# One load per group for plain v from batch 1 on, and a later place for the transposed remainders and the copies of even blocks' keys

## The chip, the cores and the metric

The kernel runs on one core of one Trainium2 chip. The core has five engines with a queue of instructions each, which they work off in order and independently of each other: TensorE (PE in the profile; its weight loads are PEld), VectorE (DVE), ScalarE (ACT), GpSimd (POOL) and SyncE (SP, which here only issues transfers). Semaphores order what one engine writes and another reads. The metric is the device time of one execution in microseconds (us), taken as the median over runs; lower is better.

## The reference

There are 8 batches, 8 heads, 576 positions and a head size of 64. Half of the heads attend to the last 32 positions ("plain"), the other half to every fourth of the last 128 ("dilated"):

```python
rel = pos[:, None] - pos[None, :]
mask_plain = (rel >= 0) & (rel < window)                              # window = 32, heads 0 to 3
mask_dil = (rel >= 0) & (rel < window * dilation) & (rel % dilation == 0)   # dilation = 4, heads 4 to 7
attn = softmax(where(mask, q @ k.T / sqrt(64), -1e9)) ; x = heads of attn @ v side by side (8, 576, 512)
gate = sigmoid(causal depthwise convolution of x, 5 taps, conv_w (5, 512))
out = (gate * (x @ w_val)) @ w_out                                    # w_val, w_out (512, 512)
```

Inputs and output are float32; the kernel works in bf16 on PE.

## The kernel before, in words

**Steps and groups.** The main loop has 32 steps `i`, four for each batch `b`. One step takes two heads of one batch; `c` (0 to 3) is the step in the batch. Steps with `c` 0 and 1 are plain, `c` 2 and 3 dilated (`dil`). Two steps of a kind form a group `g`, 16 in all; `a` is 0 in the first step of a group and 2 in the second. The lines below are those of the kernel before.

**What a step does.** The order of instructions is written out by hand in the loop (L805 to L879), and each engine keeps it; the first seven steps (`EARLY = 7`) have an order of their own in `early_rest` (L754). In a step: `scores(i, 0)` and `scores(i, 1)` (PE L494 for plain steps, L511 for dilated ones; then exp on ACT, L514); the convolution of an earlier step (PE L639, its gate on ACT L648); `apply_mask` for both halves (DVE L523), with `after_x(i-1)` between them, which transposes the normalised output of the step before (PE L593, L600, L606; DVE L608); the transposes of k or q of the next group (`trans_main`, PE L405 or L413; copied out by ACT L425 to L439); `attn_v` (PE L544 or L558); `normalize` (DVE L573, L574; L580, L581 in the first five steps); and, spread between these, value products (`run_val`: PE L664 or L659, DVE L670) and output tiles (`run_out`: PE L700, ACT L704, stores by SP L710).

**Memory for results of PE.** From step 5 on the second half of a step's scores and its attention output use the same tile `ps_sc`; there are two such tiles, so the second half of the next step's scores waits until `normalize` (L574) has read it. All else goes through four banks `ps_bank`, used in turn.

**Remainders.** A sequence has 576 = 512 + 64 positions. The main part is transposed by `trans_main`; the last 64 positions of q and k are loaded apart and transposed by `trans_rest` (two PE transposes L455; DVE copies L463 and L466 for plain groups, L473 and L475 for dilated ones). In the main loop that is done in the first step of a group, and in step 7, for the group after it, right behind `normalize`.

**Plain keys.** A plain step splits the 576 queries into six blocks of 96. A block needs its 96 keys and the 32 before them; PE takes them in two strided halves `j`. An odd block reads 128 consecutive columns of `kT`. An even block reads them likewise in batches below `FB`; from batch `FB` on it reads `kE`, in which the 96 keys of the block stand first and the 32 earlier ones behind (L490, L491). `even_keys` (L443) fills `kE` for three even blocks with two DVE copies: L447 (96 keys of each) and L448 (the 32 earlier ones of two of them; the first block has none). It depends on the main part of k alone: the columns that it reads end at 480.

**Plain v.** In batches below `FB` v is loaded by `load_v_half` (L152) in the layout of the blocks, with an overlap, 128 partitions wide: two transfers for each pair of heads. POOL then casts it to bf16 in one instruction (L219). From `FB` on v is loaded once, 96 partitions wide (L175), and POOL casts it in four pieces (L223 to L226) which move the partitions to where the blocks want them. `mask_f` and `mask_p` are the masks for the two layouts. `prep_v` does the casts; for the steps around the change POOL's order is: in step 3 `cast_val` and `prep_v(4)`, in step 4 `prep_v(5)`, `cast_out` and `prep_v(6)`, in step 5 `prep_v(7)`, in step 6 eight casts of `swap_out`.

**Loads.** SP issues all but the first few loads in program order, far ahead: in step 0 the first pair of group 2 (batch 1, plain), in step 1 its second pair, in steps 2 and 3 group 3 and group 4.

Of the kernel before, what the change touches and what calls it, by code (L numbers as in the profile page):

```python
# [15 lines left out]
def hi_bf16(ap: bass.AP) -> bass.AP:  # L16

    b = ap.bitcast(BF16)
    idx = tuple([slice(None)] * (len(b.shape) - 1) + [slice(1, None, 2)])
    return b[idx]  # L20
# [3 lines left out]
def kernel(  # L24
# [11 lines left out]
    nc = tc.nc  # L36

    B, H, S, D = q.shape
# [10 lines left out]
    NB = 6  # L49
    AVS = 72  # L50
    HB = 288
    KOFF = 32
# [33 lines left out]
    kTs = [consts.tile([128, 2, KOFF + S], BF16, name=f"kT{i}") for i in range(NKT)]  # L86

    kEs = [consts.tile([128, 2, NB // 2, 128], BF16, name=f"kE{i}") for i in range(NKT)]
    FB = 2
    NET = 2  # L90
    ets = [consts.tile([128, 2, 2 * HB + 96], BF16, name=f"et{i}") for i in range(NET)]
    NVP = 2
# [1 line left out]
    vPs = [consts.tile([128, 4, NB, 66], BF16, name=f"vP{i}") for i in range(NVP)]  # L94
# [21 lines left out]
    def bank_b():  # L116
        return bank().bitcast(BF16).rearrange("p (z n) -> p z n", z=2)
# [51 lines left out]
    def load_v(g, a=0, e=4, eng=nc.sync):  # L169
        b, dil = g // 2, g % 2  # L170
        t = grp_tiles.setdefault(g, {})
        if not dil and b >= FB:

# [36 lines left out]
    def prep_v(i):  # L210
# [3 lines left out]
        if not dil:  # L214
            w = vPst[b % NVP][:, a * NB // 2:e * NB // 2, :].rearrange(
                "p (h u) (j d) -> p h (u j) d", u=NB // 2, j=2)
            x = vPs[b % NVP][:, a:e, :, 0:D]
            if b < FB:
                nc.gpsimd.tensor_copy(x, w)  # L219
# [14 lines left out]
    def pair_info(i):  # L234
        b, c = i // NCH, i % NCH
        dil = int(c >= NCH // 2)
        return b, c, dil, 2 * b + dil, (c % 2) * 2
# [45 lines left out]
        nc.vector.memset(et[:, :, 2 * HB:], 1.0)  # L283
    for i in range(NVP):
        nc.vector.memset(vPs[i][:, :, :, D:D + 1], 1.0)
        if i == 0:
            nc.vector.memset(vPst[i][0:16, 0, :], 0.0)

# [76 lines left out]
    def make_conv_diag(c):  # L365
        nc.vector.tensor_tensor(
            out=conv_diag[:, c, :, :],
            in0=ident_h[:, None, :].to_broadcast([128, K, D]),
            in1=conv_w_sb[:, c, :, None].to_broadcast([128, K, D]),
            op=ALU.mult)  # L370
# [69 lines left out]
                    out=t["kB"][:, 2 * z0:2 * z1, 0:TM - TB, :],  # L440
                    in_=src.rearrange("p z (h w t) -> p (z h) t w", h=2, w=2)[:, :, TB:TM, :])

    def even_keys(g):  # L443
        t = grp_tiles[g]
        ke = t["kE"] = kEs[(g // 2) % NKT]
        kt = t["kT"][:, :, KOFF:KOFF + S].rearrange("p z (u s) -> p z u s", u=NB // 2)
        nc.vector.tensor_copy(ke[:, :, :, 0:96], kt[:, :, :, 0:96])  # L447
        nc.vector.tensor_copy(ke[:, :, 1:NB // 2, 96:128], kt[:, :, 0:NB // 2 - 1, 160:192])  # L448

    def trans_rest(g):  # L450
        dil = g % 2
        t = grp_tiles[g]
        ps = bank_b()
        for z in range(2):
            nc.tensor.transpose(  # L455
                out=ps[:, 0, TM * z:TM * z + TM],
                in_=hi_bf16(t["rest"][:, z, :]), identity=ident)
        pk, pq = ps[:, 0, 0:TM], ps[:, 0, TM:2 * TM]
        if not dil:
            if "qT" not in t:  # L460
                t["qT"] = qt_pool.tile([128, 2, DIL, T], BF16, name="qT")
            t["kT"] = kTs[(g // 2) % NKT]
            nc.vector.tensor_copy(  # L463
                t["kT"][:, :, KOFF + RM:KOFF + S], pk.rearrange("p (s z) -> p z s", z=2))
            for z in range(2):
                nc.vector.tensor_copy(  # L466
                    t["qT"][:, z, :, TM:T],
                    pq.rearrange("p (t r z) -> p z r t", r=DIL, z=2)[:, z])
        else:
            t["qB"] = qt_pool.tile([128, 4, 2, TR], BF16, name="qB")  # L470
            if "kB" not in t:
                t["kB"] = qt_pool.tile([128, 4, 64, 2], BF16, name="kB")
            nc.vector.tensor_copy(  # L473
                t["kB"][:, :, TM - TB:64, :], pk.rearrange("p (t w h) -> p h t w", h=4, w=2))
            nc.vector.tensor_copy(t["qB"], pq.rearrange("p (t w h) -> p h w t", h=4, w=2))  # L475
# [4 lines left out]
    def scores(i, hf):  # L480
# [3 lines left out]
        for n in range(3):  # L484
            if not dil:
                u, j = (3 * hf + n) // 2, (3 * hf + n) % 2
                for z in range(2):
                    m = 2 * u + z
                    kk = t["kT"][:, a // 2, 96 * m + j:96 * m + j + 127:2]
                    if z == 0 and b >= FB:  # L490
                        kk = t["kE"][:, a // 2, u, j:128:2]  # L491
# [25 lines left out]
    def apply_mask(i, hf):  # L517
        b, c, dil, g, a = pair_info(i)
        et = st[(i, "et")]
        e3 = et[:, hf, 0:2 * HB].rearrange("p (h n) -> p h n", h=2)  # L520
        m = mask_d if dil else (mask_f if b < FB else mask_p)[:, 3 * hf:3 * hf + 3, :].rearrange("p n q -> p (n q)")
        m = m[:, None, :].to_broadcast([128, 2, HB])
        nc.vector.tensor_tensor(out=e3, in0=e3, in1=m, op=ALU.mult)  # L523
# [195 lines left out]
    def run_conv(i):  # L719

        while convs and convs[0][0] < i:
            conv(*convs.pop(0)[1])

    def run_val():
        item = vals.pop(0)
        while item not in gates:
            conv(*convs.pop(0)[1])
        val(*item)
        G = item[2]
        done_val[G] += 1  # L730

        while HB * (done_val[G] // NCH) >= 128 * (done_out[G] + 1):
            outs.append((G, done_out[G]))
            done_out[G] += 1
# [8 lines left out]
    EARLY = 7  # L743

    def next_pair(i, names=("k", "q", "rest")):

        g, z = (i + 1) // 2, (i + 1) % 2
        for name in names:
            if name != "rest":
                trans_main(g, name, (z,))  # L750
            elif z == 0:
                trans_rest(g)

    def early_rest(i):  # L754

        if i == 0:
            setup_conv_w()
            make_conv_diag(0)
            warm(3)
        run_conv(i - 1)  # L760
        apply_mask(i, 0)
        if i == 0:
            make_conv_diag(1)
        if i > 0:
            after_x(i - 1)
        apply_mask(i, 1)
        if i == 0:
            make_conv_diag(2)
            next_pair(i, ("k",))
        elif i < NCH:  # L770
            next_pair(i)
        if i < NCH:
            warm(2)
        else:
            run_val()
        attn_v(i, 0)
        attn_v(i, 1)
        if i == 0:
            next_pair(i, ("q",))
        normalize(i)  # L780
        if i == 0:
            make_conv_diag(3)
        if i < NCH:
            warm(1)
        else:
            run_val()
            next_pair(i)
        if i == 5:
            run_val()
            run_val()  # L790
        elif i == 6:
            run_out()
            trans_main(4, "k")
            run_out()
# [10 lines left out]
    for i in range(NP):  # L805
        b, c, dil, g, a = pair_info(i)

        if i == 0:
            load_weight(0, moe_w_val)
            load_pair(2, 0)  # L810
        elif i == 1:
            load_pair(2, 2)
        elif i == 2:
            load_weight(1, moe_w_out)
            load_pair(3, 0)
        elif i == 3:
            load_pair(3, 2)
            load_group(4)
        if c % 2 == 0 and 5 <= g + 3 < 2 * B:
            load_group(g + 3)  # L820

        if i == 0:
            prep_v(0)
            make_mask_d()
            prep_v(1)
            make_perm()
        elif i < 3:
            prep_v(i + 1)
            if i == 2:
                make_mask_p()  # L830
        elif i == 3:
            cast_val()
            prep_v(4)
        elif i == 4:
            prep_v(5)
            cast_out()
            prep_v(6)
        elif i == 5:
            prep_v(7)
        elif i == 6:  # L840
            for m in range(NCH):
                for h in range(2):
                    swap_out(h, m)
        elif i > 6:
            if i < NP - 1:
                prep_v(i + 1)
            if g + 2 < 2 * B and g % 2 == 0:
                cast(g + 2, "k" if a == 0 else "q")
            if 9 <= i < 13:
                swap_val(i - 9)  # L850
        scores(i, 0)
        scores(i, 1)
        if i < EARLY:
            early_rest(i)
            continue
        run_conv(i - 1)
        apply_mask(i, 0)
        after_x(i - 1)
        if g + 1 < 2 * B:
            trans_main(g + 1, "k" if a == 0 else "q")  # L860
        apply_mask(i, 1)
        if c == 0 and outs:
            run_out()
        elif vals:
            run_val()
        attn_v(i, 0)
        attn_v(i, 1)
        normalize(i)
        if (a == 0 or i == EARLY) and g + 1 < 2 * B:
            trans_rest(g + 1)  # L870
            if dil:
                even_keys(g + 1)
        if c == 0 and vals:
            run_val()
        for _ in range((2 if len(outs) > 2 else 1) - (c == 0 and i > NCH)):
            if outs:
                run_out()
        if vals:
            run_val()  # L879
    run_conv(NP - 1)  # L880
    if outs:
        run_out()
# [36 lines left out]
```

## Time and profile before

| what | us |
|---|---|
| median of 13 runs (lowest, highest) | 180.41 (178.81, 182.33) |
| the profiled execution, whole time | 179.82 |
| its span in the profile | 177.9 |
| busy in it: PE, DVE, ACT, POOL | 162.2, 124.8, 114.0, 94.5 |
| L447, the 96 keys of each even block: least, median, most of 6 | 0.298, 0.427, 0.535 |
| L448, the 32 earlier keys of two blocks: least, median, most of 6 | 0.177, 0.184, 0.830 |
| four partial casts of v for one step, from 47.50 to 50.74 | 3.24 |
| the one cast of v for a step of batches 0 and 1 | 0.82 |

The span runs from the first to the last instruction that the profiler saw; the whole time has 1.9 us around it. The median of the runs stands 0.59 us above the profiled execution. A row of slices shows 40 equal parts of the span, 4.45 us each, in tenths. In the rows of the time line, the first number is the start within the span, the second the length of that group of instructions; "[0.36 <-ACT et L514]" says that the engine stood idle for 0.36 us before it, and what ended that. In the list of waits the numbers are the sum, how often, and the longest.

### The profile page before, as it was taken

How to read it: one execution, taken by the hardware profiler on the slowest of the kernel's cores; microseconds unless marked ns; L12 is line 12 of the kernel's file. 1: busy time of each engine (PE TensorE's matmuls, PEld its weight loads, DVE VectorE, ACT ScalarE, POOL GpSimd, SP SyncE). 2: the span in 40 equal slices, each digit the busy share in tenths (PEclk: the TensorE clock that was granted, in tenths of full speed). 3: DMA queues.
4: the chain of work that ended last, by engine and by line, in shares of the span. 5: the costliest groups of instructions: out<-in, count | busy, mean ns of one | idle time of the engine just before them, and what ended most of it. 6: DMA issues, size and time to landing. Idle time of an engine off the chain costs nothing.

```text
span 177.9 us, 7022 instructions
## 1 busy us (share of the span) xinstructions
PE 162.2 (91%) x2911; PEld 108.5 (61%) x2911; DVE 124.8 (70%) x314; ACT 114.0 (64%) x215; POOL 94.5 (53%) x164
## 2 busy tenths in 40 slices
PE   6879779789969899999999999999999999999991
PEld 2445547576546665667766676677677766665540
DVE  4397726776478798789878876887597959773330
ACT  3337724656867766777877778777967796564340
POOL 7373761559698994799069839923788100000000
PEclk9999966999999999999999999999999999999998
DMA  5999999999999999979999999999997222224355
GB/s 149 234 258 346 330 203 244 336 270 250 272 332 249 326 338 314 186 209 336 288 254 307 326 318 248 310 296 292 260 331 244 64 63 63 61 63 105 94 165 169
DMA packets 49274, 42.27 MB, mean 238 GB/s; under 512 B 6885, under 2 KB 43733, under 8 KB 49242
## 3 DMA queue, kind: packets, MB, share of 16 engines
q1 hardware_dynamic: 48544, 41.36, 86.3%
q8 instruction: 22, 0.36, 0.9%
q10 hardware_dynamic: 698, 0.47, 0.8%
q14 instruction: 10, 0.08, 0.2%
HBM read 32.38 MB, written 9.44 MB: 235 GB/s over the span
## 4 chain that ended last, share of the span: by engine, by line
PE 69%; DVE 11%; DMA 10%; ACT 4%; SPq 3%; issue 1%; ACTq 0%; DVEq 0%
PE ps_bank L700 16%; PE ps_bank L664 14%; PE ps_bank L639 11%; DMA q_nat<-in_q_dram 10%; PE ps_bank L413 5%; DVE et L523 4%; PE ps_sc L544 4%; PE ps_sc L494 3%; PE ps_sc L558 3%; PE ps_sc L511 2%; PE ps_bank L593 2%; DVE xn L574 2%; DVE xT L608 2%; PE ps_bank L606 2%; ACT et L514 1%; SPq L127 1%
## 5 line engine op out<-in xcount | busy, mean ns | idle before, releaser
L514 ACT ACTIVATE et<-ps_sc 128x576 bf16<-128x576 f32 x64 | 38.3, 648 | 16.6 <-PE ps_sc L494 11.7
L704 ACT ACTIVATE osb<-ps_bank 128x512 f32<-128x512 f32 x35 | 21.4, 611 | 25.0 <-PE ps_bank L700 18.6
L670 DVE SCALAR_TENSOR_TENSOR y<-gate,ps_bank 128x288 bf16<-128x288 bf16 x64 | 28.3, 449 | 10.2 <-PE ps_bank L664 7.6
L639 PE MATMUL ps_bank<-xT,conv_diag 64*64 64x288 bf16 (+1 forms) x768 | 27.7, 270 | 0.1
L574 DVE TENSOR_TENSOR xn<-ps_sc,rec 128x768 bf16<-128x768 f32 (+1 forms) x27 | 25.8, 955 | 0.9
L648 ACT ACTIVATE gate<-ps_bank 128x288 bf16<-128x288 f32 x64 | 23.1, 423 | 2.0 <-PE ps_bank L639 1.9
L523 DVE TENSOR_TENSOR et<-et,mask_d 128x576 bf16<-128x576 bf16 x32 | 16.6, 520 | 7.0 <-ACT et L514 7.0
L639 PEld LDWEIGHTS <-conv_diag 64*64 64x64 bf16 x768 | 19.1, 108 | 3.1 <-DVE qB L475 0.8
L664 PE MATMUL ps_bank<-xT,w_val_b 128*128 128x288 bf16 x128 | 20.4, 290 | 0.2 <-DVE xT L608 0.2
L700 PEld LDWEIGHTS <-y 128*128 128x128 bf16 x140 | 12.2, 97 | 11.3 <-DVE y L670 0.9
L700 PE MATMUL ps_bank<-w_out_b,y 128*128 128x512 bf16 x72 | 18.5, 379 | 0.0
L608 DVE COPY xT<-ps_bank 128x576 bf16<-128x576 bf16 x32 | 14.5, 454 | 5.5 <-PE ps_bank L606 3.2
L700 PE MATMUL ps_bank<-w_out_s,y 128*128 128x512 bf16 x68 | 17.5, 379 | 0.0
L206 POOL CAST k_b<-k_nat 128x512 bf16<-128x512 f32 x10 | 6.3, 656 | 19.0 <-PE ps_bank L413 11.7
L664 PE MATMUL ps_bank<-xT,w_val_s 128*128 128x288 bf16 x96 | 15.5, 285 | 0.0
L523 DVE TENSOR_TENSOR et<-et,mask_p 128x576 bf16<-128x576 bf16 x24 | 12.3, 513 | 3.6 <-ACT et L514 3.6
L664 PEld LDWEIGHTS <-w_val_b 128*128 128x128 bf16 x128 | 11.8, 99 | 3.8 <-issue 0.2
L228 POOL CAST vA<-v_st 128x512 bf16<-128x512 f32 x16 | 10.6, 664 | 5.9 <-DMA v_st<-in_v_dram 5.9
L428 ACT COPY kT<-ps_bank 128x1024 bf16<-128x1024 bf16 (+1 forms) x10 | 8.4, 845 | 6.1 <-PE ps_bank L405 5.9
L664 PEld LDWEIGHTS <-w_val_s 128*128 128x128 bf16 x96 | 9.1, 97 | 4.3
L573 DVE RECIPROCAL rec<-ps_sc 128x12 f32<-128x12 f32 (+1 forms) x27 | 6.2, 231 | 7.5 <-PE ps_sc L544 6.2
L544 PEld LDWEIGHTS <-et 64*128 64x128 bf16 x384 | 7.0, 94 | 7.2 <-DVE et L523 4.0
(120 smaller groups left out, 316.9 us busy)
## 6 DMA issues: line engine op xcount, KB each, us to landing
k_nat<-in_k_dram SPq DMA_DIRECT2D x12, 512.0 KB, 6.1
q_nat<-in_q_dram SPq DMA_DIRECT2D x12, 512.0 KB, 7.8
vPst<-in_v_dram SPq DMA_DIRECT2D x6, 576.0 KB, 8.3
v_st<-in_v_dram SPq DMA_DIRECT2D x6, 512.0 KB, 6.0
k_nat<-in_k_dram SPq DMA_DIRECT2D x8, 256.0 KB, 6.2
q_nat<-in_q_dram SPq DMA_DIRECT2D x7, 256.0 KB, 5.9
out_dram<-osb SPq DMA_DIRECT2D x7, 256.0 KB, 6.5
out_dram<-osb SPq DMA_DIRECT2D x8, 224.0 KB, 4.9
```

The costliest lines, as they stand in the source:

```text
L228: nc.gpsimd.tensor_copy(vAs[b % NVD][:, a:e, :, 0:D], t["vst"][:, a:e, :].rearrange("p h (r d) -> p h r d", r=DIL))
L514: nc.scalar.activation(out=e3, in_=ps[:, :, 0:HB], func=AF.Exp, scale=scale)
L523: nc.vector.tensor_tensor(out=e3, in0=e3, in1=m, op=ALU.mult)
L544: nc.tensor.matmul(out=ps[z][:, x * AVS:x * AVS + D + 1], lhsT=et[D * z:D * z + D, h2, col:col + 128], rhs=vPs[b % NVP][D * z:D * z + D, a ...
L574: nc.vector.tensor_tensor(out=dst, in0=av[:, :, :, 0:D], in1=rec[0:R, :, :, None].to_broadcast([R, 2, 6, D]), op=ALU.mult)
L608: nc.vector.tensor_copy(xTs[b % NXT][:, c, :, 2:], pr)
L639: nc.tensor.matmul(out=pss[G][D * hp:D * hp + D, o * T:(o + n) * T], lhsT=conv_diag[D * h:D * h + D, c, K - 1 - m, :], rhs=xt[D * h:D * h ...
L648: nc.scalar.activation(out=gate, in_=pss[G][:, 0:HB], func=AF.Tanh, scale=0.5)
L664: nc.tensor.matmul(out=ps[:, 0:HB], lhsT=w[:, mc, c * 128:(c + 1) * 128], rhs=xt[:, mc, 2 * G:2 * G + 2, 2:], start=(mc == 0), stop=(mc == ...
L670: nc.vector.scalar_tensor_tensor(out=y_half[G][:, c, b % YB * HB:(b % YB + 1) * HB], in0=gates.pop((b, c, G)), scalar=1.0, in1=ps[:, 0:HB] ...
L700: nc.tensor.matmul(out=ps, lhsT=y_half[G][:, c, y0:y0 + 128], rhs=w[:, c, :], start=(c == 0), stop=(c == NCH - 1),)
L704: nc.scalar.mul(out=osb, in_=ps, mul=0.5)
```

## The change

`FB` goes from 2 to 1, so that batch 1 is treated as the later batches are: one load of v, four casts, `mask_p`, and even blocks' keys from `kE`. The columns of v's tile that no load fills from now on are set to zero at the start. `even_keys` can do one pair of heads at a time, and steps 3 and 4 end with it for batch 1. In the main loop `even_keys` moves from behind `trans_rest` in the first dilated step of a batch (and in step 7) to behind the second mask in the second dilated step (and in step 7, there ahead of `trans_rest`). `trans_rest` moves from behind `normalize` to the end of the step, behind the value products and output tiles.

```diff
-    FB = 2
+    FB = 1
...
         nc.vector.memset(vPs[i][:, :, :, D:D + 1], 1.0)
+        if i >= FB:
+            nc.vector.memset(vPs[i][32:64, :, 0:2, 0:D], 0.0)
...
-    def even_keys(g):
+    def even_keys(g, z0=0, z1=2):
         t = grp_tiles[g]
         ke = t["kE"] = kEs[(g // 2) % NKT]
-        kt = t["kT"][:, :, KOFF:KOFF + S].rearrange("p z (u s) -> p z u s", u=NB // 2)
-        nc.vector.tensor_copy(ke[:, :, :, 0:96], kt[:, :, :, 0:96])
-        nc.vector.tensor_copy(ke[:, :, 1:NB // 2, 96:128], kt[:, :, 0:NB // 2 - 1, 160:192])
+        kt = t["kT"][:, z0:z1, KOFF:KOFF + S].rearrange("p z (u s) -> p z u s", u=NB // 2)
+        nc.vector.tensor_copy(ke[:, z0:z1, :, 0:96], kt[:, :, :, 0:96])
+        nc.vector.tensor_copy(
+            ke[:, z0:z1, 1:NB // 2, 96:128], kt[:, :, 0:NB // 2 - 1, 160:192])
...
             run_val()
             next_pair(i)
+        if i in (3, 4):
+            even_keys(2, i - 3, i - 2)
         if i == 5:
...
         apply_mask(i, 1)
+        if dil and a and g + 1 < 2 * B:
+            even_keys(g + 1)
...
         normalize(i)
-        if (a == 0 or i == EARLY) and g + 1 < 2 * B:
-            trans_rest(g + 1)
-            if dil:
-                even_keys(g + 1)
         if c == 0 and vals:
             run_val()
...
         if vals:
             run_val()
+        if (a == 0 or i == EARLY) and g + 1 < 2 * B:
+            trans_rest(g + 1)
```

The engines' instructions move as follows. PE, in the main loop: the two transposes L455 change places with the value products and output tiles that stood behind them. DVE: the copies L463, L466 (or L473, L475) come behind the value products' L670; L447 and L448 go from behind them to between the second mask and `normalize`, one step later; two half-size pairs of key copies come new, behind `normalize` of step 3 and at the end of step 4. POOL: eight partial casts for two whole ones. SP: two loads for four. ACT: nothing moves.

## The prediction

> **What bounds the kernel now.** I read the page first, then the list of waits of PE, then the time line around the places that the diff touches.
>
> ```profile
> span 177.9 us, 7022 instructions
> PE 162.2 (91%) x2911; PEld 108.5 (61%) x2911; DVE 124.8 (70%) x314; ACT 114.0 (64%) x215; POOL 94.5 (53%) x164
> ...
> PEclk9999966999999999999999999999999999999998
> DMA  5999999999999999979999999999997222224355
> ...
> PE 69%; DVE 11%; DMA 10%; ACT 4%; SPq 3%; issue 1%; ACTq 0%; DVEq 0%
> ```
>
> PE carries the chain; DMA is busy to about 138 us but holds only 10% of the chain, all of it before 24 us (its last link is a q load that lands at 23.93). After that PE never waits for a load. So one us of PE idle is one us of time, and bytes saved after 24 us are worth nothing by themselves. The waits of PE from 24 to 51 us show where idle is left:
>
> ```profile
> PE ps_sc L494 <- DVE kE L447: 1.1, 1, 1.1
> PE ps_bank L405 <- DMA q_nat<-in_q_dram: 1.0, 1, 1.0
> PE ps_sc L494 <- ACT qT L425: 0.7, 1, 0.7
> PE ps_bank L659 <- ACT kB L439: 0.6, 1, 0.6
> PE ps_sc L494 <- DVE kE L448: 0.5, 1, 0.5
> ```
>
> The two kE lines are one place, scores of step 8 at 50 us, 1.59 us together. From 70 us on the stages have PE busy for all or nearly all of their length.
>
> Next, the end of step 3 and the start of step 4 on PE, DVE and POOL (start, length, engine, line):
>
> ```profile
> 26.91 0.69 PE L494 MATMUL ps_sc<-qT,kT 64*64 64x96 bf16 x24
> ...
> 27.18 0.56 DVE L581 TENSOR_TENSOR xn<-ps_bank,rec 128x384 bf16<-128x384 f32 x1
> 28.10 0.46 DVE L523 TENSOR_TENSOR et<-et,mask_f 128x576 bf16<-128x576 bf16 x1 [0.36 <-ACT et L514]
> ...
> 26.85 0.83 POOL L219 CAST vP<-vPst 128x768 bf16<-128x768 f32 x1 [1.93 <-DMA vPst<-in_v_dram]
> 31.28 0.82 POOL L219 CAST vP<-vPst 128x768 bf16<-128x768 f32 x1 [3.60 <-DMA vPst<-in_v_dram]
> ```
>
> The reader is to see that PE starts step 4's scores at 26.91, before DVE has finished normalising step 3 (27.74), and that POOL has one 0.83 us cast here and then rests. Last, the key copies and the casts of the kind that batch 1 is to get:
>
> ```profile
> 49.64 0.40 DVE L447 COPY kE<-kT 128x576 bf16<-128x576 bf16 x1
> 49.96 0.83 DVE L448 COPY kE<-kT 128x128 bf16<-128x128 bf16 x1
> ...
> 49.05 0.82 POOL L225 CAST vP<-vPst 32x768 bf16<-32x768 f32 x1
> 49.92 0.82 POOL L226 CAST vP<-vPst 32x768 bf16<-32x768 f32 x1
> ```
>
> L448 takes 0.18 where POOL rests (median 184 ns) but 0.83 here: it ends at 50.79, right behind POOL's cast at 50.74. A cast on POOL holds off a key copy.
>
> **What the skill says.** The Trainium skill, "SBUF — State Buffer", section "Who interferes with whom": VectorE shares one pair of ports with GpSimd as an exclusive lock; a copy in a two-port mode, or an operation with two SBUF inputs, blocks for the whole of the other's instruction. The L448 above agrees, and so does the mask product L523 (two SBUF inputs): 0.45 us alone, 0.70 at 33.97 and 39.75 beside casts. "TensorE: Matmul & The Clock Gate", Part 1, says that the clock is halved after an idle window of about 3.4 us and restored only after a busy one. The trace agrees in kind: granted clock 0.50 from about 23.6 to 30.0 us, after PE had worked 1.05 of the 3.0 us from 20.6 to 23.6. The same page, "Step-by-step", says that matmuls stay in program order: whatever stands behind a waiting score matmul waits too.
>
> **The change part by part.**
>
> *1. Loads.* Batch 1's plain v takes two loads of 96x6x512 B (295 KB) for four of 64x6x512 B (197 KB): 0.2 MB and two issues of about 0.7 us on SP saved, after the last load that PE waits for. At the 270 GB/s of that stretch later loads land up to 0.7 us sooner. No one on PE waits for them: 0. At most it brings POOL's first cast from 26.85 to about 26.5.
>
> *2. POOL.* Steps 4 and 5 get the four partial casts for one: from the rows at 47.50, 0.60+0.82+0.82+0.82 with gaps is 3.24 us, against 0.83. That is 2.4 us more, twice. POOL is then busy from about 26.7 to 30 and 31 to 34. Step 4's vP is wanted at 30.26 and step 5's at 34.77, both later if PE is later; w_out (wanted at 42.6) ends about 37.3 for 36.5. No direct wait: 0, but the cover of a quiet POOL is gone for DVE.
>
> *3. Key copies in step 3.* They stand behind L581 (end 27.74), in front of step 4's scores, which now read kE for half of their matmuls. Full copies take 0.30 and 0.18 unblocked, 0.40 as a pair; for half-size ones I estimate 0.3. Bound below: first score at about 27.95 for 26.91, so +1.0. Above: the first copy waits for a cast until about 28.4, and the second for the next one to 29.2, as at 49.96. The ninth matmul, which needs the second copy, ran at about 27.1: +2.1. Behind it in PE's queue stand conv, the x transposes, val and step 4's attention. I take **+1.6**.
>
> *4. Key copies in step 4.* They follow the k transposes and ACT's copy (31.79 to 32.37) and DVE's y (to 32.67); step 5's scores started at 32.92, held by the q copy. Unblocked +0.1 to 0.2; with both copies blocked +1.4. I take **+0.6**.
>
> *5. Four masks beside casts.* 0.25 us each by the rows above, of which the second of step 4 and those of step 5 release PE: **+0.3** (0 to 0.8).
>
> *6. Step 7, copies ahead of normalise.* The 1.59 us wait disappears in its old form, but the score's second half needs the bank freed by L574 and the last needs the remainders (L463, L466). Copies start after the mask at 47.58. Beside POOL they take about 1.4, so L574 moves from 48.31 to about 49.3, ends at 50.3, and the remainders end at 50.75: the scores end at 50.95 for 51.05. With POOL quiet they would end near 49.9. I take **-0.3** (0 to -1.2).
>
> *7. Steps 11, 15, 19, 23, 27.* The copies leave the first step of each dilated group, which has room, for the second. There L574 frees the bank of the next step's second half of scores just in time:
>
> ```profile
> 105.48 0.96 DVE L574 TENSOR_TENSOR xn<-ps_sc,rec 128x768 bf16<-128x768 f32 x1
> ...
> 106.61 0.21 PE L494 MATMUL ps_sc<-qT,kE 64*64 64x96 bf16 x2
> ```
>
> It ends at 106.44; DVE has 0.11 idle before y; the pair is 0.40. Slack is 0.17 less some 0.05 for the signal: 0.40-0.11-0.12 is 0.17 a step, up to 0.75 beside a cast. Five steps, one or two of them partly blocked: **+0.9** (0.5 to 2.0).
>
> *8. Remainders at the end of a step.* PE's two transposes swap places with val and out: same sum, and the scores behind them do not read the result for a step. On DVE y comes first, the copies after; the bank that conv waited for 0.2 us (PEld L639 on L475) is now freed by y at about the same time. Hidden by the wait for exp (0.47 us before the mask at 103.28). With the copies out of the first step, the 0.27 us wait of PE for the mask at 68.25 should go: **-0.2** (0 to -0.5).
>
> *9. The extra memset*, some 0.3 us on DVE at 3 us, lies under DVE's idle from 4 to 6: 0.
>
> Sum: 1.6+0.6+0.3-0.3+0.9-0.2 = +2.9 us on the profiled 179.82 (span 177.9 and 1.9 around it), which is 182.7. The median of the 13 runs is 0.59 above that execution; so I forecast 180.41+2.9 = 183.3.
>
> **Rivals.**
> *Clock.* The stall of item 3 falls into the stretch 26.6 to 30.0 after which PE got its clock back. If it leaves that window too idle, PE stays at half speed for one more, about 3.3 us, of which 1.6 is lost: +4.4, so 184.8. For it: a stretch with PE busy 88% of the time, 23.6 to 26.8, did not restore the clock. Against: the window's place is not ours to choose, and slower PE hides part of items 4 and 5.
> *Light.* Casts and copies miss each other: 1.0+0.2+0-0.6+0.7-0.3 = +1.0, so 181.4.
> *Not slower.* The wait at 50 us is the one that counts: with the copies out of normalise-to-scores all 1.59 go, and PE's 0.7 and 0.4 idle at 32 and 35 us absorb most of the early stall, as ACT and DVE run ahead in it. 1.0+0.2-1.1-1.6+0.9-0.3 = -0.9 at its best (179.5), and -0.35 with half of the 1.1 absorbed: about 180.1. It decides once the early stall that survives is below about 1 us. Against: those idles are links of PE-ACT-PE and move with PE, and item 6's bank is still freed by L574.
>
> **Numbers.** Measurement can tell about 0.5%, or 0.9 us. Forecast (182.0 to 184.3) 0.52; clock 0.22; light 0.12, half of it inside 0.5%; not slower 0.14, of which 0.05 is faster by more (item 6 at its best as well as all the rest). So faster 0.05, within 0.5% 0.06+0.09 = 0.15, slower 0.52+0.22+0.06 = 0.80. The range 180.9 to 185.5 leaves out the last case (0.14) and, at the top, a clock case with item 3 at its upper bound (some 0.06).
>
> **What would show it.** Right: PE idle of 1 to 2 us before the scores of step 4, put down to kE; L448's kind at 0.8 there; after step 7 no wait for kE but one for L574 or the remainders; short waits of scores for L574 in five later steps; the clock row's two sixes kept or lengthened. Wrong: scores of step 4 within 0.3 us of DVE's and PE's old order, or PE's wait at 50 us gone with nothing in its place.

## The result, and the profile after

| | before | changed | changed, run again |
|---|---|---|---|
| median of the runs, us (number) | 180.39 (48) | 182.72 (11) | 182.64 (6), beside 180.64 (59) of before |
| difference of the medians, us | | +2.33 | +2.00 |
| ratio of the times, 95% interval | | 1.0181 [1.0146, 1.0216] | 1.0133 [1.0061, 1.0205] |
| profiled execution: whole time, span, us | 179.82, 177.9 | 183.53, 181.7 | 181.22, 179.4 |

The change makes the kernel about 1.3 to 1.8% slower; 183.3 was forecast. Most single executions lie within 2 us of their kernel's median, some 3 and more. The ratio leaves out executions more than 1.5% above the fastest of their kernel, so that one very fast execution shifts it, and it differs by up to 0.9% from the quotient of the medians. Both are given below, and little is built on what only one of them shows.

The line numbers of the changed kernel are two or three higher: the key copies are L449 and L450 (L447 and L448 before), the scores of plain steps L497 (L494), the masks L526 (L523), `normalize` L577 (L574).

From the page of the changed kernel: span, busy times, clock and the shares of the chain that ended last.

```profile
span 181.7 us, 7047 instructions
PE 163.1 (90%) x2911; PEld 110.0 (61%) x2911; DVE 128.4 (71%) x319; ACT 114.8 (63%) x215; POOL 98.7 (54%) x170
...
PEclk9999955899999999999999999999999999999998
...
PE 65%; DVE 15%; DMA 10%; ACT 3%; SPq 3%; issue 2%; ACTq 0%; DVEq 0%
```

PE does the same work (163.1 us for 162.2), and the chain has moved to DVE: 15% for 11%. Its waits, from PE's list for the changed kernel (sum, times, longest):

```profile
PE ps_sc L497 <- DVE xn L577: 2.0, 4, 0.9
...
PE ps_sc L497 <- ACT qT L427: 1.3, 2, 0.9
PE ps_sc L561 <- DVE et L526: 1.1, 3, 0.6
PE ps_sc L497 <- DVE kE L449: 1.0, 1, 1.0
```

The wait for kE, 1.59 us in front of step 8 before, is now 1.04 us in front of step 4, and waits of plain scores for `normalize` are new, four times. The places, in the time line of the changed kernel (start, length, engine, line; in brackets the wait of the engine):

```profile
27.40 0.56 DVE L584 TENSOR_TENSOR xn<-ps_bank,rec 128x384 bf16<-128x384 f32 x1
27.87 0.30 DVE L449 COPY kE<-kT 128x288 bf16<-128x288 bf16 x1
28.10 0.16 DVE L450 COPY kE<-kT 128x64 bf16<-128x64 bf16 x1
...
28.23 0.29 PE L497 MATMUL ps_sc<-qT,kE 64*64 64x96 bf16 x2 [1.04 <-DVE kE L449]
...
27.25 0.82 POOL L224 CAST vP<-vPst 48x768 bf16<-48x768 f32 x1
28.13 0.82 POOL L225 CAST vP<-vPst 32x768 bf16<-32x768 f32 x1
...
50.74 0.93 DVE L449 COPY kE<-kT 128x576 bf16<-128x576 bf16 x1
51.59 0.63 DVE L450 COPY kE<-kT 128x128 bf16<-128x128 bf16 x1
52.13 0.22 DVE L576 RECIPROCAL rec<-ps_sc 128x12 f32<-128x12 f32 x1
52.39 0.96 DVE L577 TENSOR_TENSOR xn<-ps_sc,rec 128x768 bf16<-128x768 f32 x1
...
53.40 0.23 PE L497 MATMUL ps_sc<-qT,kE 64*64 64x96 bf16 x2 [0.89 <-DVE xn L577]
...
50.55 0.95 POOL L226 CAST vP<-vPst 32x768 bf16<-32x768 f32 x1
51.56 0.61 POOL L223 CAST vP<-vPst 32x512 bf16<-32x512 f32 x1
...
107.31 0.71 DVE L449 COPY kE<-kT 128x576 bf16<-128x576 bf16 x1
107.94 0.38 DVE L450 COPY kE<-kT 128x128 bf16<-128x128 bf16 x1
...
109.87 0.23 PE L497 MATMUL ps_sc<-qT,kE 64*64 64x96 bf16 x2 [0.44 <-DVE xn L577]
```

Three places. At 28 us the half-size copies take 0.30 and 0.16, hardly more than the 0.25 and 0.17 that they take in E6 below with POOL idle, and step 4's scores stand 1.04 us all the same, since the copies come behind two normalisations. At 51 us the copies do run beside POOL's casts, take 0.93 and 0.63, and push L577 to 52.39; step 8's second half of scores waits for its bank until 53.40. At 107 us a smaller form of the same thing costs 0.44.

### The profile page after: what moved, and what is told of

Read it like the earlier page. It is cut to its first block, busy times and chain, and to the rows that moved or that the text cites. A ratio compares the mean times of both kernels' runs of the same rounds, so it can differ in the third digit from the quotient of the medians.

```text
span 181.7 us, 7047 instructions
## 1 busy us (share of the span) xinstructions
PE 163.1 (90%) x2911; PEld 110.0 (61%) x2911; DVE 128.4 (71%) x319; ACT 114.8 (63%) x215; POOL 98.7 (54%) x170
## 4 chain that ended last, share of the span: by engine, by line
PE 65%; DVE 15%; DMA 10%; ACT 3%; SPq 3%; issue 2%; ACTq 0%; DVEq 0%
PE ps_bank L703 14%; PE ps_bank L667 12%; PE ps_bank L642 11%; DMA q_nat<-in_q_dram 10%; PE ps_bank L415 5%; DVE et L526 4%; PE ps_sc L547 4%; DVE xn L577 3%; PE ps_sc L497 3%; PE ps_bank L662 3%; PE ps_bank L596 3%; PE ps_sc L514 2%; PE ps_sc L561 2%; DVE xT L611 2%; SPq L127 2%
## 5 line engine op out<-in xcount | busy, mean ns | idle before, releaser
L577 DVE TENSOR_TENSOR xn<-ps_sc,rec 128x768 bf16<-128x768 f32 (+1 forms) x27 | 25.8, 956 | 0.9
L526 DVE TENSOR_TENSOR et<-et,mask_d 128x576 bf16<-128x576 bf16 x32 | 17.2, 536 | 6.8 <-ACT et L517 6.3
L526 DVE TENSOR_TENSOR et<-et,mask_p 128x576 bf16<-128x576 bf16 x28 | 15.5, 555 | 3.5 <-ACT et L517 3.5
L225 POOL CAST vP<-vPst 32x768 bf16<-32x768 f32 x14 | 12.3, 875 | 0.9
L226 POOL CAST vP<-vPst 32x768 bf16<-32x768 f32 x14 | 12.3, 882 | 0.6
L223 POOL CAST vP<-vPst 32x512 bf16<-32x512 f32 x14 | 8.7, 622 | 7.3 <-PE ps_sc L514 3.2
```

The costliest lines, as they stand in the source:

```text
L225: nc.gpsimd.tensor_copy(x[64:96], w[32:64])
L226: nc.gpsimd.tensor_copy(x[96:128], w[64:96])
L577: nc.vector.tensor_tensor(out=dst, in0=av[:, :, :, 0:D], in1=rec[0:R, :, :, None].to_broadcast([R, 2, 6, D]), op=ALU.mult)
```

## The experiments

All times below are in us. E1 to E4 ran beside 43 runs of the kernel before (median 180.46), E5 to E8 beside 45 (180.51), the last four beside 59 (180.64).

### E1: the loop's edits alone

Batch 1 stays in pairs; only the moves in the main loop (and `even_keys` for a part of the heads, not used here) are made.

```diff
-    FB = 1
+    FB = 2
...
-        if i in (3, 4):
-            even_keys(2, i - 3, i - 2)
```

> Only the edits in the main loop: the remainders at the end of a step, the key copies behind the second mask one step later (and in step 7 ahead of normalise); v, masks and the scores of batch 1 as before. Theory A (two independent costs: key copies in front of batch 1's scores, and key copies in front of normalise in the main loop): about +0.9 us over before, ratio 1.004 to 1.008; steps 15 to 25 lose 0.2 to 0.5 us each where a GpSimd cast runs beside the copies, step 8 waits for L577's counterpart in place of kE. Rival B (all of the loss is batch 1's new layout, the loop edits are harmless): ratio 0.998 to 1.002, no wait of scores for the normalised tile.

Measured: median 179.51 (22 runs), ratio 0.987 [0.9833, 0.9906]. The loop's edits make the kernel faster, where the first theory expected a small loss and the rival no change. One place where it wins is step 7, in this kernel's time line:

```profile
46.81 0.30 DVE L449 COPY kE<-kT 128x576 bf16<-128x576 bf16 x1
47.03 0.19 DVE L450 COPY kE<-kT 128x128 bf16<-128x128 bf16 x1
...
47.62 0.96 DVE L577 TENSOR_TENSOR xn<-ps_sc,rec 128x768 bf16<-128x768 f32 x1
...
47.18 0.61 POOL L223 CAST vP<-vPst 32x512 bf16<-32x512 f32 x1 [1.55 <-DMA vPst<-in_v_dram]
```

The same two copies, at the same place in DVE's order, take 0.30 and 0.19 because the first cast of the next v starts only at 47.18, when its load lands. Nothing waits in front of step 8. Of the later steps, three wait for L577, 0.81, 0.41 and 0.46, which is 1.68 and as much as the 1.59 that went. So the waits of scores in this profile do not account for the gain.

Part of it may be the clock. Each execution has its mean granted clock and its span on record, and the traces show no granted clock but half and full, so the time at half speed can be worked out as (1 - clock) x span / 0.5. E1's 22 executions average 4.9 us of it, the 43 of the kernel before beside them 7.7. Over 147 executions of the kernel before, each us at half speed goes with 0.26 us more time; by that, an estimate, 0.7 of E1's gain. Why its executions had less is open.

### E2: batch 1's layout alone, with the old loop

```diff
-    FB = 2
+    FB = 1
...
+        if i in (3, 4):
+            even_keys(2, i - 3, i - 2)
```

> Only batch 1's new layout (one load of v, four casts, mask_p, key copies at the end of steps 3 and 4); the main loop in its old order. Theory A: about +2.3 us, ratio 1.011 to 1.015, with PE idle for about 1 us before step 4's scores and the scores of step 8 waiting 1 to 1.6 us for kE as before. Rival B: the whole loss, ratio 1.016 to 1.021.

Measured: median 182.32 (6 runs), +1.9, with no ratio; that is nearer to the first theory, but with six runs from 179.13 to 183.25 not clear of either. Scores wait for kE 1.59 in front of step 4, 1.34 in front of step 5 (1.13 and 0.21) and 1.26 in front of step 8, so the first two are the layout's, and the third is the old one. In this execution step 3's first copy took 0.85 beside a cast that began just before it, so the first wait is longer than in the changed kernel.

### E3: the changed kernel with step 3's key copies earlier

Step 3's copies come right behind the transposes of the keys, ahead of those of the queries, instead of at the end of the step.

```diff
+        elif i < NCH:
+            next_pair(i, ("k",))
+            even_keys(2, 0, 1)
+            next_pair(i, ("q", "rest"))
...
-        if i in (3, 4):
-            even_keys(2, i - 3, i - 2)
+        if i == 4:
+            even_keys(2, 1, 2)
```

> The changed kernel, but step 3's key copies stand right behind that step's k transposes, ahead of its remainders, where VectorE stands idle for some 3 us; nothing else moves. Theory A: PE's 1.04 us wait before step 4's scores goes, and PE's clock comes back at 30 us and not at 33, which is another 0.5 to 1.0: ratio 1.006 to 1.012. Rival C (the four casts on GpSimd and the masks beside them hold PE, the place of the copies does not matter): ratio 1.016 to 1.020.

Measured: median 181.82 (22 runs), +1.36, ratio 0.9986 [0.9944, 1.0028]. The wait in front of step 4 is gone. The next consumers are the row of this kernel's time line below and step 4's attention, which now waits 0.64 for the cast L226.

```profile
33.13 0.23 PE L497 MATMUL ps_sc<-qT,kE 64*64 64x96 bf16 x2 [1.02 <-DVE kE L449]
```

By the medians a third or so of the loss went (+1.36 for +2.0 to +2.3), as the first theory had it; by the ratio all of it. That the wait goes with the place of the copies is clear, what it is worth is not.

### E4: the changed kernel with the loop's copies behind `normalize`

```diff
         apply_mask(i, 1)
-        if dil and a and g + 1 < 2 * B:
-            even_keys(g + 1)
...
         normalize(i)
+        if dil and a and g + 1 < 2 * B:
+            even_keys(g + 1)
```

> The changed kernel, but in the main loop (and step 7) the key copies stand behind normalise in place of ahead of it. Theory A: the waits of scores for the normalised tile in steps 16, 20 and 24 (0.21, 0.44, 0.45 us) and in step 8 (0.89) go, in step 8 one for kE of 0.5 to 1.0 comes back: -1.1 to -1.6 us against the changed kernel, ratio 1.009 to 1.013. Rival B: no difference to the changed kernel, ratio 1.016 to 1.020.

Measured: median 185.15 (6 runs), +4.7, ratio 1.0225 [1.0148, 1.0301]. L577 is early again, but the copies now stand directly in front of the scores that read them. From PE's list of waits for this kernel:

```profile
PE ps_sc L497 <- DVE kE L449: 4.3, 7, 1.1
...
PE ps_sc L497 <- DVE kE L450: 1.2, 4, 0.5
```

Both expectations missed: no gain came, and the kernel is slower than the changed one. So putting the copies one step later leaves no good place at the end of that step: ahead of `normalize` they delay a bank, behind it the keys themselves.

### E5: the changed kernel with PE kept busy during the wait

Four matmuls whose result nobody reads stand between steps 3 and 4, in place of one.

```diff
-        if i < NCH:
+        if i == NCH - 1:
+            ps = bank()
+            for _ in range(4):
+                nc.tensor.matmul(out=ps, lhsT=junk[:, 0:128], rhs=junk, start=True, stop=True)
+        elif i < NCH:
```

> The changed kernel with four matmuls on a filled tile in place of one at the end of step 3, so that PE has work while step 4's scores wait for the key copies (1.04 us). Theory D (the idle PE keeps its half clock for one more window of some 3.2 us): the clock is back near 30 us in the trace and 0.5 to 1.2 us are won against the changed kernel, ratio to before 1.006 to 1.011. Theory A without the clock (only the wait itself costs): no gain, 1.012 to 1.019, the wait for kE replaced by the matmuls.

Measured: median 182.27 (22 runs), +1.76, ratio 1.0043 [1.0007, 1.0079]. The medians say that nothing was won, the ratio that one per cent was. The profiled execution had full clock before and behind the added matmuls, so it doesn't show what they do to the clock: inconclusive.

### E6 and E7: batch 1's two halves of the work apart

Both have the old loop. E6 keeps the loads in pairs and copies and reads kE for batch 1; E7 loads singly, casts in four pieces and lets batch 1's even blocks read `kT`, without key copies.

E6, with `FB = 2` and the copies at the end of steps 3 and 4:

```diff
-                    if z == 0 and b >= FB:
+                    if z == 0 and b >= 1:
...
+        if i in (3, 4):
+            even_keys(2, i - 3, i - 2)
```

E7, without those copies:

```diff
-    FB = 2
+    FB = 1
...
-                    if z == 0 and b >= FB:
+                    if z == 0 and b >= 2:
```

> Of the change only the key copies: batch 1's scores read kE, filled at the end of steps 3 and 4; v's loads, its one cast, the masks and the main loop are those of before. The even blocks' keys of batch 1 then stand in another order than its mask and v take them, so that part of the computation is not that of the reference. Theory A (key copies in front of the scores): +1.1 to 1.7 us, ratio 1.006 to 1.010, PE idle for about 1 us before step 4's scores. Rival C (the casts on GpSimd are what costs): 0.998 to 1.003.

> Of the change only v: batch 1's v by single loads, four casts a step, the mask for that layout; its scores read kT as before and no keys are copied for it, so the even blocks' keys of batch 1 do not match the mask and v; the main loop is that of before. Theory A: +0.2 to 0.8 us for masks beside casts, ratio 1.001 to 1.005, no wait of PE before step 4's scores. Rival C: +1.8 to 2.5 us, ratio 1.010 to 1.014.

Measured: E6 183.4 (6 runs), +2.9, ratio 1.0179 [1.013, 1.0228]; E7 180.63 (14 runs), +0.1, ratio 1.0019 [0.9984, 1.0054]. The key copies of steps 3 and 4 carry the cost of the layout; eight casts for two, one DMA layout for another and longer masks cost nothing that can be measured (the interval leaves room for 0.5%). E6 lies above both of its expected ranges. Its six executions average 11.4 us at half speed, 4.6 more than the kernel before beside them, uncertain by 2.6; at 0.26 each that is 1.2 of its 2.9, an estimate.

### E8: key copies where nothing waits

Batch 1 in pairs, remainders at the end of a step, the loop's copies in the first dilated step behind `normalize`, and step 8's in step 6, behind the transposes of its keys (the first line of the diff). The diff is against the kernel before.

```diff
+            even_keys(4)
...
         normalize(i)
-        if (a == 0 or i == EARLY) and g + 1 < 2 * B:
-            trans_rest(g + 1)
-            if dil:
-                even_keys(g + 1)
+        if dil and a == 0 and g + 1 < 2 * B:
+            even_keys(g + 1)
...
+        if (a == 0 or i == EARLY) and g + 1 < 2 * B:
+            trans_rest(g + 1)
```

> Batch 1 as before (two-load layout). In the main loop the remainders stand at the end of a step; the key copies stay in the first dilated step behind normalise; those for step 8 stand in step 6, behind the k transposes, where VectorE waits 3.2 us for exp. Theory A (what counts is whether the copies stand in front of something that PE asks for soon): faster than before by 1.0 to 2.0 us, ratio 0.989 to 0.995, no wait for kE or for the normalised tile in steps 16, 20, 24. Rival E (the gain of the loop edits comes from moving the copies one step later, which this undoes): 0.996 to 1.003.

Measured: median 179.62 (14 runs), -0.9, ratio 0.9966 [0.9915, 1.0018]. No plain score waits for kE or L577, as the first theory had it. The time does not decide: the median is just short of that theory's 1.0, and the ratio lies in the rival's range.

### The changed kernel again

> The changed kernel once more, beside the three that follow, so that its ratio stands on the same chip as theirs. Expected 1.012 to 1.020 of the kernel before.

Measured: +2.00, ratio 1.0133, as in the table above. Its profile differs in the clock. From its page, span and clock:

```profile
span 179.4 us, 7047 instructions
...
PEclk9979999999999999999999999999999999999999
```

The half-speed stretch lies earlier, from 8.1 to 11.5, and is 3.4 us long instead of 10.2; there is none in the steps of the change, and the span is 2.3 shorter than in the first profile. The waits are there nevertheless (PE rows of its time line):

```profile
26.66 0.23 PE L497 MATMUL ps_sc<-qT,kE 64*64 64x96 bf16 x2 [1.41 <-DVE kE L449]
32.14 0.23 PE L497 MATMUL ps_sc<-qT,kE 64*64 64x96 bf16 x2 [0.75 <-DVE kE L449]
...
49.73 0.23 PE L497 MATMUL ps_sc<-qT,kE 64*64 64x96 bf16 x2 [0.88 <-DVE xn L577]
...
106.52 0.23 PE L497 MATMUL ps_sc<-qT,kE 64*64 64x96 bf16 x2 [0.67 <-DVE xn L577]
```

### E9: E1 with the key copies ahead of the first mask

The diff is against E1; its first line is step 6, behind the transposes of step 8's keys, its second and third stand ahead of the masks.

```diff
+            even_keys(4)
...
+        if dil and a and i != EARLY and g + 1 < 2 * B:
+            even_keys(g + 1)
...
         apply_mask(i, 1)
-        if dil and a and g + 1 < 2 * B:
-            even_keys(g + 1)
```

> Both batches loaded in pairs as before; remainders at the end of a step; the loop's even-block key copies ahead of the first mask of the second dilated step instead of behind the second mask, and those of step 8 in step 6 behind the transposes of the keys. Theory A (what a copy costs is decided by what TensorE asks for next behind it; the first masks come while TensorE still has the second head's scores to do, so the copies stand beside work): 0.988 to 0.996, and no wait of a first score for normalise in step 8. Rival (a copy ahead of the first mask holds up the probabilities, and the values' matmuls wait for them in every odd second step): 0.998 to 1.004, with a wait of 0.3 to 0.6 us of L561-like value matmuls for the mask in five steps.

Measured: median 179.46 (22 runs), -1.2, ratio 0.9975 [0.9944, 1.0006]. The first theory has its missing wait; of the rival's waits for the mask there are two behind copies, 0.48 in step 11 and 0.37 in step 15 (beside casts the copies took 0.63 and 0.83 in front of the mask at 64.48). The ratio lies between the two ranges. By its waits this is a better place than behind the second mask, though not a free one; in time it can't be told from E1.

### E10: batch 1 loaded singly, with all key copies out of the way

The diff is against the changed kernel. Step 3's copies stand as in E3; step 4's keys are transposed ahead of its last value product and copied behind its `normalize`; the rest is as in E8.

```diff
+        elif i < NCH:
+            next_pair(i, ("k",))
+            even_keys(2, 0, 1)
+            next_pair(i, ("q", "rest"))
+        elif i == NCH:
+            next_pair(i, ("k",))
...
+        if i == NCH:
+            even_keys(2, 1, 2)
...
-            next_pair(i)
-        if i in (3, 4):
-            even_keys(2, i - 3, i - 2)
+            next_pair(i, ("q",) if i == NCH else ("k", "q", "rest"))
...
+            even_keys(4)
...
-        if dil and a and g + 1 < 2 * B:
-            even_keys(g + 1)
...
+        if dil and a == 0 and g + 1 < 2 * B:
+            even_keys(g + 1)
```

> Batch 1 loaded singly as in the changed kernel, but its key copies out of the way of the scores: step 3's right behind the transposes of the keys, step 4's behind transposes of the keys that are moved to the middle of step 4, ahead of its last out-projection; the loop's copies in the first dilated step behind normalise, remainders at the end, step 8's copies in step 6. Theory A (the single loads cost only what their key copies do in front of scores): 0.993 to 1.000, and no wait of more than 0.3 us of a score for kE in the trace. Rival (the layout itself costs, through the casts on GpSimd and the later half of the loads): 1.006 to 1.012 although those waits are gone.

Measured: median 179.45 (22 runs), -1.2, ratio 0.9978 [0.9943, 1.0012]. No plain score waits for kE, and the ratio lies in the first theory's range: with the key copies out of the way the layout itself costs nothing that can be measured. It has one bill left, in step 4's attention (PE row of its time line):

```profile
30.00 0.53 PE L547 MATMUL ps_bank<-vP,et 64*128 64x65 bf16 x23 [1.55 <-POOL vP L226]
```

The four casts end behind the scores that are no longer late. With that wait it still ends where E8 and E9 do.

### E11: one move in the kernel before

Step 8's key copies are made in step 6, behind the transposes of its keys, instead of at the end of step 7.

```diff
+            even_keys(4)
...
-            if dil:
+            if dil and i != EARLY:
                 even_keys(g + 1)
```

> The kernel before with one edit: the key copies of step 8 are made in step 6, behind the transposes of its keys, instead of at the end of step 7. Theory A (the wait of 1.59 us in front of step 8's first scores is where the whole gain of the loop's edits comes from): 0.992 to 0.997. Rival (that wait is only handed on to the wait behind it, and the gain comes from the remainders at the end of a step): 0.999 to 1.002, with a wait of 0.8 us or more for normalise or a mask in front of step 8 instead.

Measured: median 179.10 (22 runs), -1.5, ratio 0.997 [0.9938, 1.0002]. The copies, in its time line, lie in two us of idle DVE time and are not held up much:

```profile
45.49 0.46 DVE L447 COPY kE<-kT 128x576 bf16<-128x576 bf16 x1 [2.12 <-ACT kT L428]
45.87 0.18 DVE L448 COPY kE<-kT 128x128 bf16<-128x128 bf16 x1
```

No score waits in front of step 8, for normalise or anything else, as the first theory had it; the rival's wait of 0.8 is absent. The median sits at the size of the wait that was removed, 1.59, though the ratio gives only 0.3% of the time, at the edge of the first theory's range and with 1 just inside its interval.

### All of them beside their waits

The waits of plain scores (rows of L494 or L497 on DVE and ACT in each kernel's list of PE's waits, added up; one execution each) against the medians:

| kernel | waits of plain scores | less 2.9 of before | median less before's |
|---|---|---|---|
| changed | 4.5 | +1.6 | +2.3 |
| changed, again | 5.4 | +2.5 | +2.0 |
| E1 loop alone | 3.0 | +0.1 | -1.0 |
| E2 layout alone | 4.8 | +1.9 | +1.9 |
| E3 step 3's copies early | 3.8 | +0.9 | +1.4 |
| E4 copies behind `normalize` | 6.1 | +3.2 | +4.7 |
| E5 junk matmuls | 4.4 | +1.5 | +1.8 |
| E6 keys alone | 4.0 | +1.1 | +2.9 |
| E7 casts alone | 2.7 | -0.2 | +0.1 |
| E8 | 0.9 | -2.0 | -0.9 |
| E9 | 1.1 | -1.8 | -1.2 |
| E10 | 0.9 | -2.0 (and +1.5 for the cast) | -1.2 |
| E11 | 1.1 | -1.8 | -1.5 |

Eleven of thirteen rows agree within 1.2 in size, and the order of the kernels is nearly that of their waits. E4 and E6 are longer by 1.5 and 1.8 than their score waits say, E8 by 1.1, and E1 is shorter by 1.1. The mean time at half speed is within 1.7 us of that of the kernel before in all but three of them: E1 and E9 have 2.8 and 2.7 less, E6 has 4.6 more, with an uncertainty of 1.3 to 1.5 for the first two and 2.6 for E6.

## Why the prediction was right

The forecast was +2.9, from a sum of small items; measured is +2.3 and +2.0. The direction and the places of the loss were right: of the signs that were named, the wait for kE in front of step 4, the wait for L577 in place of that for kE in front of step 8, and waits for L577 in three and four of the five later steps are there; the second copy held up for 0.8 in front of step 4 is not. That the sum came so near is in part luck: items 3 to 6 were put too high and items 7 and 8 too low.

**Item 3, copies in front of step 4 (+1.6, from 1.0 to 2.1): mechanism right, size above what the traces have.** The waits are 1.04 and 1.41. In both profiles the copies are hardly held up (0.30 and 0.16; 0.33 and 0.16), so the upper case, copies held back by casts, did not come; the lower bound's working is what happened. E2's execution has the middle case: a copy of 0.85 beside a cast, and a wait of 1.59. E3 shows that the copies' place is the cause: moved, the wait goes.

**Item 4 (+0.6): about nothing, because it was counted beside a wait that was already there.** Step 5's scores wait 0.94 for the query copy in one profile and 0.75 for kE in the other, where they waited 0.73 for the query copy before. In E2 and E4 they wait 1.34, which is the 0.6 of the forecast.

**Items 1, 2, 5 and 9: right about their price, incomplete about what they set off.** E7 measures loads, casts and masks together at +0.1 (ratio 1.0019, interval from 0.9984 to 1.0054) against +0.3. But item 1 let later loads land "up to 0.7 us sooner" and saw nobody waiting. SP issues the load of v for step 8 at 39.02 before and in E1 at 38.56, with the single loads at 37.78, 37.23 and 36.25 (changed again, changed, E7). The casts of it start earlier in the step: 0.4 to 1.6 after step 7's first score (changed, changed again, E7) instead of 2.4 and 2.8 (before, E1). That is enough to bring them over step 7's key copies. The earlier issue is only one reason. In the first profile the load landed no earlier than before (47.87 for 47.35), but step 7 began 2.5 us later; and in E6, whose loads are the old ones, the casts start 0.2 ahead of step 7's first score, because that step began 2.7 later. So loads that land sooner and a PE that comes later both do it, and the runs do not part their shares.

**Item 6 (-0.3, from -1.2 to 0): the trade was right, the gain -0.7.** The wait for kE of 1.59 became one of 0.89 for L577, in four executions of kernels with both halves of the change (changed, changed again, E3, E5: 0.89, 0.88, 0.89, 0.89). The quiet case of -1.2 that item 6 named is E1: with batch 1 in pairs the copies finish just as the first cast starts, and nothing waits. The Trainium skill, "SBUF — State Buffer", section "Who interferes with whom", has the reason in one sentence: "Issue order, not op shape, decides who blocks." E1 and the changed kernel are that sentence measured: the same copies at 0.30 and 0.19 with the cast behind them, 0.93 and 0.63 with it ahead.

**Item 7 (+0.9, from 0.5 to 2.0): right, at the upper half.** L577's waits in the five later steps add up to 1.10 and 1.70 in the two profiles (0.21, 0.44, 0.45; 0.35, 0.22, 0.67, 0.46) and 1.68 in E1. Where POOL is quiet there is none, as in two of the steps of the first profile.

**Item 8 (-0.2): not seen.** E8, which has later remainders, is no faster than E11, which hasn't (179.62 and 179.10); nothing here shows that moving them brings or costs anything.

With the measured values, items 3, 4, 6 and 7 make 1.0 + 0.2 - 0.7 + 1.1 = 1.6 in the first profile and 1.4 + 0 - 0.7 + 1.7 = 2.4 in the second, around both results. What the sum did not price is that the two halves of the change are not independent. Alone, each is cheaper by the medians than its items: the layout +1.9 in E2 (items 1 to 5: +2.5), the loop's edits -1.0 in E1 (items 6 to 8: +0.4). Added they make +0.9, measured together +2.0 to +2.3. The 1.1 to 1.4 between are no larger than their uncertainty, about 1.8 from the spread of the executions, and E1's part has the clock in it. What shows the dependence is the traces, one execution each: from step 7's first score to step 9's, E1 takes 1.44 less than before, but changed again, E3 and E5 take only 0.32 or 0.33 less, and the first profile 0.14 more. In between lies the wait of 0.89: the layout brings the casts over the copies, and with that goes most of the loop's gain at this place. Item 6 counted on casts beside the copies, as they came; item 1's "No one on PE waits for them: 0" holds for the layout alone, and not beside copies that stand ahead of `normalize`.

**The rivals.** *Clock* did happen in the first profile, as the two stretches below show (length; PE busy and others; third last, the granted clock). Before:

```profile
23.60:26.80 3.20, 2.83 (x25) 1.60 (x25) 1.06 (x5) 0.61 (x2) 1.32 (x3) 0.50 1.17 204
26.80:30.00 3.20, 3.20 (x58) 2.41 (x58) 1.82 (x6) 1.90 (x4) 0.83 (x1) 0.50 1.12 224
30.00:33.20 3.20, 2.45 (x71) 1.66 (x73) 2.58 (x7) 1.07 (x2) 0.82 (x1) 0.99 1.07 337
```

Changed:

```profile
26.80:30.00 3.20, 2.16 (x49) 1.39 (x48) 1.93 (x6) 1.19 (x2) 2.85 (x4) 0.50 1.07 255
30.00:33.20 3.20, 3.14 (x41) 2.01 (x38) 2.13 (x6) 0.71 (x2) 2.65 (x4) 0.50 1.11 349
```

With PE busy 2.16 instead of 3.20, the clock comes back at 33 instead of 30. But it isn't what the change costs: the second profile of the same kernel has no such stretch in these steps, and the medians of the two sets agree. Over all executions the time at half speed, worked out as under E1, averages 6.7 us in 18 of the changed kernel and 7.1 in 147 of the kernel before, a difference uncertain by about 2; at 0.26 us each that can be half a us of the 2.0 to 2.3, either way. *Not slower* failed at the point that it named, the bank freed by L577; its step "with the copies out of normalise-to-scores all 1.59 go" came true only without the new layout. *Light* had the copies escape the casts everywhere; they did at 28 us and not at 51.

**What stays open.** Why E4 loses 1.5 more than its score waits; its time at half speed, 8.5 us for 7.7 before, is worth 0.2 of it. For E6's 1.8 the clock has an estimate of 1.2, but why its executions had so much of it is not known, nor why E1 and E9 had so little. Whether E5's matmuls help. And whether E8 to E11 differ: their medians lie within 0.5 of each other, with ratios of 0.9966 to 0.9978. Each is 0.9 to 1.5 below the kernel before by the medians, and each interval of the ratio reaches 1.000 to 1.002; of them, E11 needs a single move.

## What to carry to other kernels

A short copy on an in-order engine costs what the next consumer behind it waits, not what it takes: a pair of copies, some half a microsecond long, by the medians took 1.5 us off the kernel before when it was moved to where its engine idled (E11), and six such pairs put 2.4 to 2.7 on the changed kernel when they were moved behind `normalize` (E4), so put them where their engine idles and their input has just come, rather than as late as they may be. Price two edits together as well as apart: here the one, whose loads and casts cost nothing by themselves, brought a neighbour's work over the copies that the other had moved, and took back most of what that had won in one place. And where a sum is made of waits, subtract the wait that stands at the same place already.

## What the runs showed of the hardware

- VectorE's key copies for a whole group take as little as 0.30 and 0.18 us with GpSimd quiet and up to 0.93 and 0.85 beside its casts. Whether the casts began 2.8 us behind step 7's first score (E1) or 0.4 to 1.4 behind it (changed, changed again, E3, E5) decided which, and a bank, and so PE, waited not at all or 0.89.
- The half-speed stretches of PE come in steps of about 3.4 us. Ahead of the kernel's last microseconds, one of 3.4 stands in E1, E7, E9 and changed again, two in E3; one of 6.8 in before, E2 and E11, with one of 3.4 beside it in E4 and E10; one of 10.2 in changed, E6 and E8; none in E5. The same kernel had 10.2 once, from 23.1, and 3.4 once, from 8.1. The Trainium skill, "TensorE: Matmul & The Clock Gate", section "Part 1: The HAM clock gate (the "warmup" mystery)", calls the window free-running and run-variable and gives 3413 ns for it; these lengths agree. How busy PE must be for the clock to come back doesn't come out: cut from their end into lengths of 3.4, the last pieces have PE busy 89 to 100% and the pieces ahead of them 53 to 85%, but in E8 the two pieces ahead of the last, at 7.8 and 11.3, have 100 and 96%.
- Over 147 executions of the kernel before, the time at half speed averages 7.1 us, each us of it goes with 0.26 us more time, and it accounts for about a third of the spread (correlation 0.56).
- Single stops of PE of 0.6 to 0.7 us that the profile puts down to nothing ("issue") stand at a different place in each of several executions: 60.52 in the changed kernel, 76.36 in E1, 90.21 in E8, 110.64 in E11. Differences of single profiles below a microsecond late in the kernel therefore say little.
